# Attention and expert layer on one core: two buffers of turned x, batch 3 turned a slot sooner, x asked for ahead of row stores, batch 0's logits later, states @ w1 behind a slot's small pieces

## The chip, the cores and the metric

The kernel runs on one core of a Trainium2 chip. The metric is the device time of one execution in microseconds, from measurement outside the profile; the profile gives the span from the first to the last instruction of one profiled execution. The engines are TensorE (PE), VectorE (DVE), ScalarE (ACT), GpSimd (POOL) and SyncE (SP), which here issues nearly all the loads. Each engine works through its own queue in order and waits on semaphores for the others.

## The reference

```python
# x [8, 8, 512, 64], state [8, 8, 32, 64]   (batch, head, rows, D)
scores  = 0.125 * x @ state^T               # softmax over the 32 states
xread   = softmax(scores) @ state           # 512 rows per batch
scores2 = 0.125 * state @ x^T               # softmax over the 512 rows of x
sread   = softmax(scores2) @ x              # 32 rows per batch
tok = concat([xread, sread], axis=2).transpose(0, 2, 1, 3).reshape(8 * 544, 512)

logits = tok @ w_gate                       # 8 experts
e      = argmax(logits, axis=1)             # one expert per token
gate   = softmax(logits)[token, e]
out[token] = gate * (relu(tok @ w1[e]) @ w2[e])   # 512 -> 1024 -> 512
```

All of it is in float32. `w1` and `w2` are 2 MB for each expert.

## The kernel before

**What is computed.** The 512 x rows of a batch all go through one expert, the one that most of them choose, found at run time (`count`, `most`, `eb`, read by SP into a register with `expert_of`, and used as the address of the weight loads). The state rows are sorted by expert and go through their own rounds at the end; the token rows that did not choose their batch's expert are done in a branch behind all else. The x rows of the attention read are never formed: as `xread @ w1 = softmax @ (state @ w1)`, `states_w1` computes G = state @ w1 (PSUM tiles `pG`, 32 products for a batch, copied to `G` by ScalarE), and `up` multiplies the softmax weights, transposed (`aT`), by G (`ph`). `down` multiplies relu's output `hT` by w2 (`py`, 8 products of 128 x 512 for each of 4 chunks c); batches 2 to 7 use a seven-product scheme in `down_by_halves` and `up_by_halves`.

**The order of the work.** Everything is issued through one wrapper (line 48) that keeps each engine in program order, so every row of the profile shows L48 and has to be told apart by its tiles. The program's order is written by hand. `batch(b)` (line 1088) issues `down` of batch b and `up` of batch b+1; in between stand *slots* (`slots`, line 1129), into which the attention work of later batches is cut. One step of a slot issues one or two weight loads waiting in `lazy`, and one step of `attention()` (line 1063), which advances each running generator by one piece. In batch 0, `down` has slots 0 to 7: two for each chunk c, one behind the fourth `py` product of the chunk and one behind the chunk's store; `up(1)` has slots 8 to 11, `down(1)` slots 12 to 19. `between(c)` (line 1092) issues the `pG` of the next batch just ahead of a slot: with c = 2 in batch 0 ahead of slot 5, with c = 1 in batch 1 ahead of slot 15.

**The pieces.** `stages(b)` (line 335) is the attention of one batch, cut at each `yield`: turn x and the states (`turn_x`, `xt`; `turn_states`, `stT`, copied on by GpSimd); the gates of the states and first half of the scores (`states_gates`, `pg`; `scores`, `pc`); the second half, and the transposes and maxima on VectorE (`sx`, `mx`, `nm`); the exponentials (`a2`, `sx`); the transposed weights of the x read (`turn_read`, `aT`, which is also stored to `at_dram`); the transposed weights of the state read (`turn_write`, `pt`, `a2T`); the state rows and the logits of the x rows (`write_rows`, `pw`, `xs`; `logits_x`, `pl`, `lg`, and `route` on VectorE); the turned state rows (`turn_rows`, `pxs`); and the choice of the expert with the state rows' logits (`choose`, `count`, `pr`, `cnt`; `logits_s`, `pls`, `lgs`). From slot 0 on, a batch begins every third slot, batch 2 in slot 0. `begin()` (line 431) does batch 0's attention and batch 1's start, the latter in `beside()`, three steps taken between the `ph` of batch 0's last two chunks. `first()` (line 1034) is what is left of batches 0 and 1 and takes slots 0 to 6: `write_rows(0)`; `turn_write(1)`; `logits_x(1)`; `choose(1)` and the load of batch 1's w1; `write_rows(1)`; `turn_rows` of both; `logits_s` of both.

**Buffers.** Four PSUM banks (`bank`, tag p) are shared in turn by `py`, `ph`, `pG`, `pg`, `pt`, `pw`, `pl`, `pls`, `pxs` and `pr`; a new tile waits until the last reader of the bank it gets is done. The other four banks hold one `pc`. `xt` has one buffer for the whole of a batch, filled by two transposes; `x_nat` has three. `fetch_batch(b + 3)` at the end of `write_rows(b)` asks for x and the states three batches on, behind the four stores of the state rows to `srow`. SP waits, for each DMA it issues, for the one eight earlier.

Of the kernel before, what the change touches and what calls it, by code (L numbers as in the profile page):

```python
# [9 lines left out]
FP32 = mybir.dt.float32  # L10
# [10 lines left out]
def kernel(  # L21
# [34 lines left out]
    B, H, S, D = x.shape  # L56
# [142 lines left out]

    NB = 8  # L200

    def turn_x(b, xt, h):
        dve.transpose(xt[:, h].rearrange("p h c u t -> p (h c u t)"),
                      x_nat[b][:, h].rearrange("p h c d -> p (h c d)"))

    def turn_states(b, copy):

# [17 lines left out]
    def scores(b, xt, pc, g):  # L225

        for u in range(2):
            for q in range(4):
                for i in range(4):
                    pe.matmul(pc[ts(q, 32), i, ts(g, 128)], lhsT=stT[b][ts(i, 32), 2 * q + g, u ^ (i % 2), :],  # L230
                              rhs=xt[ts(i, 32), 2 * q + g, :, u, :],
                              start=(u == 0), stop=(u == 1), skip_group_check=True)

    def turn_scores(pc, sx, i):
# [37 lines left out]
    def new_pc():  # L272
        return ps_c.tile([128, 4, 512], FP32, tag="c", name="pc")

    def new_xt():
        return att.tile([128, H, NC, 2, 32], FP32, tag="xt", bufs=1, name="xt")

    def new_sx():
        return att.tile([128, 4, NB, NS], FP32, tag="sx", bufs=2, name="sx")
# [16 lines left out]
    def write_rows(b):  # L296

        _, _, s2, a2T = soft[b]
        pw = bank("pw")[:, 0:128].rearrange("p (g d) -> p g d", g=2)
        for g in range(2):  # L300
            for c in range(NC):
                for q in range(4):
                    pe.matmul(pw[ts(q, 32), g], lhsT=a2T[:, g, c, ts(q, 32)], rhs=x_nat[b][:, 2 * q + g, c, :],
                              start=(c == 0), stop=(c == NC - 1), skip_group_check=True)
        xs = rows_of[b] = att.tile([128, 2, D], FP32, tag="xs", bufs=2, name="xs")
        for g in range(2):
            act.activation(xs[:, g], pw[:, g], AF.Copy, scale=s2[:, g:g + 1])
        for q in range(4):
            sp.dma_start(out=srow[ts(b % 4, NS), b // 4, ts(q, 128)], in_=xs[ts(q, 32)].rearrange("p g d -> p (g d)"))
        fetch_batch(b + 3)  # L310

    def fetch_batch(b):
        if b < B:
            load_x(b, sp)
            load_states(b, sp, sp)

    def turn_read(b, i=ALL):
        if b not in aT:
            aT[b] = att.tile([128, 4, 2, 128], FP32, tag="aT", bufs=NE, name="aTe")[:]
        dve.transpose(aT[b][:, i].rearrange("p i g s -> p (i g s)"),  # L320
                      soft[b][0][:, i].rearrange("p i b n -> p (i b n)"))
        if i.stop == 4:
            sp.dma_start(out=at_dram[b], in_=aT[b].rearrange("p i g s -> p (i g s)"))

    def logits_x(b):
        pl = bank("pl")[:, 0:128]
# [7 lines left out]

    def stages(b):

        xt, sx = new_xt(), new_sx()
        turn_x(b, xt, slice(0, 4))
        turn_x(b, xt, slice(4, 8))
        turn_states(b, gp.tensor_copy)  # L340
        yield
        states_gates(b)
        pc = new_pc()
        scores(b, xt, pc, 0)
        yield
        scores(b, xt, pc, 1)
        for i in range(4):
            turn_scores(pc, sx, i)
        less_max(sx, ALL, gp)
        nm = write_max(pc)  # L350
        yield
        soft[b] = (sx,) + write_weights(pc, nm)
        exponential(sx, ALL)
        over_sum(sx, ALL, gp)
        yield
        turn_read(b)
        yield
        turn_write(b)
        yield
        write_rows(b)  # L360
        exps, gates = logits_x(b)
        yield
        exps()
        xsT = turn_rows(b)
        yield
        choose(b)
        logits_s(b, xsT)
        gates()

    def turn_rows(b):  # L370
# [4 lines left out]
        act.copy(xsT[:].rearrange("p q n -> p (q n)"), pt[:, 0:128])  # L375
        return xsT

    def logits_s(b, xsT):

        pl = bank("pls")[ts(b % 4, 32), 0:E]  # L380
        for q in range(4):
            pe.matmul(pl, lhsT=xsT[:, q, :], rhs=wg[:, q, :], start=(q == 0), stop=(q == 3), skip_group_check=True)
        dve.tensor_copy(out=lgs[ts(b % 4, 32), b // 4], in_=pl)
# [47 lines left out]
    def begin():  # L431
# [13 lines left out]
        most(0, pr)  # L445
        keep_warm(9)
        turn_states(0, act.copy)
        xt, sx = new_xt(), new_sx()
        turn_x(0, xt, slice(0, 4))
        e = expert_of(eb, 0)  # L450
        at_once(w1_parts(0, e, 2))
        load_x(1, sp)
# [1 line left out]
        sp.dma_start(out=wg[:], in_=moe_w_gate.rearrange("(c p) e -> p c e", p=128))  # L454
        at_once(w2_parts(0, e))
        fetch_batch(2)
        turn_x(0, xt, slice(4, 8))
        pc = new_pc()
        for g in range(2):
            scores(0, xt, pc, g)  # L460
# [27 lines left out]
        up(G, aT[0], hT, one, fs=far)  # L488
        up(G, aT[0], hT, two, fs=far)
        nm = write_max(pc)  # L490
        xt, sx = new_xt(), new_sx()
        turn_x(1, xt, slice(0, 4))
        turn_x(1, xt, slice(4, 8))
        turn_states(1, gp.tensor_copy)
        first_e = att.tile([1, 1], FP32, name="first_e")
        dve.tensor_copy(out=first_e[:], in_=eb[0:1, 0:1])
# [1 line left out]
        def beside():  # L498
            nonlocal nm, pc
            soft[0] += write_weights(pc, nm)  # L500
            states_gates(0)
            yield
            states_gates(1)
            pc = new_pc()
            scores(1, xt, pc, 0)
            yield

            pr = bank("pre")[:, 0:1]
            pe.matmul(pr, lhsT=ones_f[0:1].to_broadcast([1, 128]), rhs=first_e[:], start=True, stop=True)
            scores(1, xt, pc, 1)  # L510
            exps, gates = logits_x(0)
            dve.tensor_copy(out=eb[:, 0:1], in_=pr)
            for i in range(4):
                turn_scores(pc, sx, i)
            less_max(sx, ALL, dve)
            nm = write_max(pc)
            early.append(stages(2))
            next(early[0])
            yield
            exps()  # L520
            gates()
            count(0)
            turn_write(0)
            exponential(sx, ALL)
            soft[1] = (sx,) + write_weights(pc, nm)
            over_sum(sx, ALL, dve)
            turn_read(1)
            yield
# [505 lines left out]
    def first():  # L1034

        write_rows(0)
        yield
        turn_write(1)
        yield
        exps, gates = logits_x(1)  # L1040
        yield
        exps()
        choose(1)
        e1 = expert_of(eb, 1)
        at_once(w1_parts(1, e1))
        lazy.extend(w2_parts(1, e1))
        gates()
        yield
        write_rows(1)
        yield  # L1050
        xsT = [turn_rows(b) for b in range(2)]
        yield
        for b in range(2):
            logits_s(b, xsT[b])

    def advance(gens, which):
        for g in which:
# [5 lines left out]
    def attention():  # L1063

        gens, slot = [first()], 0
        while gens:
            b = 2 + slot // 3
            old, new = gens[:], slot % 3 == 0 and b < B
            begun = slot < 6
            if begun:  # L1070
                advance(gens, old[:1])
            if new:
                gens.append(early.pop() if early else stages(b))
                if b > 2:
                    next(gens[-1])
            advance(gens, old[1:] if begun else old)
            slot += 1
            yield
# [9 lines left out]
    def batch(b):  # L1088

        nonlocal G, hT  # L1090

        def between(c):
            nonlocal G
            if c == (1 if b else 2) and b + 1 < B:
                G = states_w1(new_G(), w1s[b + 1], stG[:, b + 1])
            yield
            if c == 1 and 0 < b < B - 2:
                lazy.extend(w1_parts(b + 2, expert_of(eb, b + 2)))
            yield

        def between_products(n):
            nonlocal G
            if n in (3, 4) and b + 1 < B:
                if n == 3:
                    G = new_G()
                states_w1(G, w1s[b + 1], stG[:, b + 1], (n - 3,),
                          lambda name: late["ps_t"].tile([128, 512], FP32, tag="t", bufs=2, name=name))
            yield
            if n == 4 and b + 2 < B:
                lazy.extend(w1_parts(b + 2, expert_of(eb, b + 2)))  # L1110
            if n == 5 and b + 1 < B:
                sums_of[b + 1] = up_sums(G, aT[b + 1])
            yield

        if b < NE:
            down(hT, w2s[b], store_batch(b), slots, between)
        else:
            down_by_halves(b, hT, w2s[b], slots, between_products)
        if 0 < b < B - 2:
            lazy.extend(w2_parts(b + 2, expert_of(eb, b + 2)))  # L1120
        if b + 1 in sums_of:
            hT = up_by_halves(G, aT[b + 1], sums_of[b + 1], new_hT(), slots)
        elif b + 1 < B:
            hT = up(G, aT[b + 1], new_hT(), insert=slots, at=(1, 3, 5, 7) if b + 1 < NE else (1, 3, 4, 5, 6, 7))
        if b == 0:
            e2 = expert_of(eb, 2)
            lazy.extend(w1_parts(2, e2) + w2_parts(2, e2))
# [127 lines left out]
```

## Time and profile before

| | us |
|---|---|
| median of 4 runs | 444.74 (444.41 to 445.6) |
| the profiled execution | 444.26 |
| its span | 440.0 |
| PE busy | 428.7 |
| DVE busy | 225.2 |
| POOL busy | 153.3 |
| ACT busy | 127.4 |

The profiled execution has 4.26 us around its span. The granted clock of TensorE has a mean of 0.997 of full speed. The DMA engines move 110 MB, 250 GB/s on the mean.

A row of the profile's timeline gives the start and the length in us, the engine, the line, the operation, and output tiles <- input tiles with their shapes; behind xN, N instructions are put together. Brackets hold the time that the engine had stood idle and what released it. In the list of waits, the columns are the total, the number of times and the longest. A busy share that is high over the whole span can hide where the idle time lies; the forty slices and the tables by stretch show that.

### The profile page before, as it was taken

To read this page: it belongs to the slowest core of one execution; us is meant where nothing else is said; L and a number is where in the kernel's file an instruction comes from. 1 tells how busy PE (TensorE), PEld (TensorE's weight loads), DVE (VectorE), ACT (ScalarE), POOL (GpSimd) and SP (SyncE) were. 2 spreads that over 40 slices of the span, in tenths; PEclk is the share of its full clock that TensorE was granted. 3 is DMA by queue.
4 is the path that set the end of the run, shared out by engine and by line. 5 is a ranking of instruction groups with operands and counts; after the bars stand their busy time and mean duration, and the time that the engine had idled before them with its cause. 6 is when DMAs were issued, how large, how long until landed. Compare 5 with 4: busy or idle time off the path is not lost.

```text
span 440.0 us, 10186 instructions
## 1 busy us (share of the span) xinstructions
PE 428.7 (97%) x3933; PEld 290.9 (66%) x3933; DVE 225.2 (51%) x482; ACT 127.4 (29%) x287; POOL 153.3 (35%) x143
## 2 busy tenths in 40 slices
PE   8899989999999999999999999999999999999995
PEld 7676544555555457786758677766867685768673
DVE  4667784787796657433505261523442370527151
ACT  1454233453343442212311241012340242025100
POOL 2010140412422431673327424534336253644231
PEclk9999999999999999999999999999999999999998
DMA  5990289565493454899999699779937998884211
GB/s 180 330 336 11 94 266 331 162 217 160 127 368 107 148 204 142 268 347 403 385 388 385 196 338 393 271 269 397 387 143 236 395 373 285 307 285 170 95 49 59
DMA packets 64514, 110.04 MB, mean 250 GB/s; under 512 B 12944, under 2 KB 22416, under 8 KB 64465
## 3 DMA queue, kind: packets, MB, share of 16 engines
q1 hardware_dynamic: 60240, 99.99, 65.9%
q0 software_dynamic: 2240, 7.08, 4.2%
q10 hardware_dynamic: 1984, 2.31, 1.5%
q8 instruction: 32, 0.52, 0.5%
q14 instruction: 18, 0.14, 0.1%
HBM read 94.15 MB, written 14.95 MB: 248 GB/s over the span
## 4 chain that ended last, share of the span: by engine, by line
PE 85%; DVE 9%; DMA 2%; SPq 1%; issue 1%; POOL 1%; ACT 1%; DVEq 0%; POOLq 0%
PE ph L48 22%; PE pD L48 10%; PE pX L48 10%; PE py L48 7%; PE pY L48 5%; PE pZ L48 5%; PE pgy L48 5%; PE pgh L48 5%; PE pW L48 5%; PE pG L48 3%; PE pc L48 3%; DVE sx L48 2%; DVE xt L48 2%; DMA st<-in_state_dram 2%; PE pt L48 1%; DVE sm L48 1%
## 5 line engine op out<-in xcount | busy, mean ns | idle before, releaser
L48 PE MATMUL py<-w2t,hT 128*128 128x512 f32 x128 | 59.0, 604 | 0.0
L48 DVE TENSOR_TENSOR hT<-ph,hT 128x512 f32<-128x512 f32 x50 | 34.6, 692 | 40.7 <-PE ph L48 40.7
L48 POOL TENSOR_TENSOR Ta<-w2t,Ta 128x1024 f32<-128x1024 f32 x12 | 30.6, 2546 | 46.6 <-PE pD L48 26.7
L48 PE MATMUL pX<-w2t,hT 128*128 128x256 f32 x192 | 43.7, 381 | 0.0
L48 PEld LDWEIGHTS pX<-w2t,hT 128*128 128x128 f32 x192 | 36.2, 190 | 6.4 <-issue 1.7
L48 PEld LDWEIGHTS py<-w2t,hT 128*128 128x128 f32 x128 | 23.0, 189 | 25.6 <-issue 24.9
L48 DVE SCALAR_TENSOR_TENSOR yh<-pY,gw,yh 128x256 f32<-128x256 f32 x24 | 10.0, 478 | 54.3 <-PE pY L48 47.8
L48 ACT ACTIVATE hT<-ph 128x512 f32<-128x512 f32 (+2 forms) x50 | 22.9, 462 | 41.0 <-PE ph L48 41.0
L48 PE MATMUL ph<-aTl,G 128*128 128x256 f32 (+1 forms) x112 | 33.8, 444 | 0.0
L48 PE MATMUL ph<-aTe,G 128*128 128x128 f32 (+2 forms) x128 | 30.4, 388 | 1.4 <-DVE aTe L48 1.2
L48 ACT ACTIVATE yh<-pX,gw 128x256 f32<-128x256 f32 x36 | 14.4, 473 | 53.8 <-PE pX L48 52.6
L48 POOL DMA_DIRECT2D out_dram<-yh x23 | 16.8, 731 | 33.5 <-DVE yh L48 16.9
L48 POOL TENSOR_TENSOR sx<-sx,mx 128x1024 f32<-128x1024 f32 x6 | 11.5, 1912 | 47.1 <-DVE mx L48 47.1
L48 ACT ACTIVATE hT<-hT 128x512 f32<-128x512 f32 x30 | 18.9, 630 | 30.7 <-DVE hT L48 30.7
L48 PEld LDWEIGHTS ph<-aTl,G 128*128 128x128 f32 x112 | 20.6, 190 | 9.6 <-issue 7.7
L48 PEld LDWEIGHTS ph<-aTe,G 128*128 128x128 f32 x128 | 18.8, 191 | 10.2 <-issue 6.7
L48 ACT COPY G<-pG 128x512 f32<-128x512 f32 x32 | 17.0, 591 | 23.9 <-PE pG L48 23.9
L48 PE MATMUL pY<-Ta,Sa 128*128 128x256 f32 x96 | 22.2, 384 | 0.0
L48 POOL COPY stT<-stT 64x512 f32<-64x512 f32 x7 | 4.2, 606 | 51.5 <-DVE first_e L48 20.7
L48 PE MATMUL pZ<-Tb,Sb 128*128 128x256 f32 x96 | 22.1, 383 | 0.0
L48 PEld LDWEIGHTS pY<-Ta,Sa 128*128 128x128 f32 x96 | 17.8, 190 | 6.4 <-issue 3.4
L48 POOL TENSOR_TENSOR Tb<-w2t 128x1024 f32<-128x1024 f32 x6 | 14.2, 2371 | 22.2 <-issue 22.2
(176 smaller groups left out, 745.3 us busy)
## 6 DMA issues: line engine op xcount, KB each, us to landing
s<-in_moe_w_dram SPq DMA_DIRECT2D x192, 256.0 KB, 6.0
w2t<-in_moe_w_dram SPq DMA_DIRECT2D x32, 512.0 KB, 7.0
w1t<-in_moe_w_dram SPq DMA_DIRECT2D x28, 512.0 KB, 6.2
x_nat<-in_x_dram SPq DMA_DIRECT2D x16, 512.0 KB, 6.5
out_dram<-yh POOLq DMA_DIRECT2D x23, 256.0 KB, 5.2
at_dram<-aTl SPq DMA_DIRECT2D x6, 512.0 KB
w1t<-in_moe_w_dram SPq DMA_DIRECT2D x2, 1024.0 KB
out_dram<-y ACTq DMA_DIRECT2D x8, 256.0 KB, 6.2
```

Source lines behind the costliest of these rows:

```text
L48: ins = getattr(self.engine, name)(*args, **kw)
```

## The change

The change moves work; the instructions are nearly the same.

1. `xt` is two half tiles instead of one whole, with one pair in the attention pool for even batches, and one for odd batches in tiles (`Sa`, `Sb`) that batches 2 and up use later. Turning a batch no longer has to wait for the scores of the batch before it.
2. Batch 3 is turned in slot 2 instead of slot 3, behind the transposed weights of batch 1 on VectorE's queue.
3. `write_rows` asks for x and the states three batches on ahead of the four row stores; the store of batch 1's `aT` moves from `turn_read(1)` to behind `write_rows(0)`.
4. In `beside()`, `logits_x(0)` moves one step later, ahead of `turn_write(0)`; `count(0)` moves to slot 0, behind `write_rows(0)`; batch 2 is turned after the exponentials.
5. The two `logits_s` of batches 0 and 1 write to one PSUM bank, in different partitions of it.
6. In `between(c)`, the `pG` products stand behind the slot's pieces instead of ahead of them (slot 5 for batch 1, slot 15 for batch 2).

```diff
-    def turn_x(b, xt, h):
-        dve.transpose(xt[:, h].rearrange("p h c u t -> p (h c u t)"),
-                      x_nat[b][:, h].rearrange("p h c d -> p (h c d)"))
+    def turn_x(b, xt, k):
+
+        dve.transpose(xt[k][:].rearrange("p h c u t -> p (h c u t)"),
+                      x_nat[b][:, ts(k, 4)].rearrange("p h c d -> p (h c d)"))
...
-    def new_xt():
-        return att.tile([128, H, NC, 2, 32], FP32, tag="xt", bufs=1, name="xt")
+    def new_xt(b):
+
+        return [(att, ffn)[b % 2].tile([128, 4, NC, 2, 32], FP32, tag=("xt0", "xt1", "Sa", "Sb")[2 * (b % 2) + k], name="xt")
+                for k in range(2)]
...
+        fetch_batch(b + 3)
         for q in range(4):
             sp.dma_start(out=srow[ts(b % 4, NS), b // 4, ts(q, 128)], in_=xs[ts(q, 32)].rearrange("p g d -> p (g d)"))
-        fetch_batch(b + 3)
...
-        if i.stop == 4:
-            sp.dma_start(out=at_dram[b], in_=aT[b].rearrange("p i g s -> p (i g s)"))
+        if i.stop == 4 and b != 1:
+            keep_read(b)
+
+    def keep_read(b):
+        sp.dma_start(out=at_dram[b], in_=aT[b].rearrange("p i g s -> p (i g s)"))
...
-    def logits_s(b, xsT):
-
-        pl = bank("pls")[ts(b % 4, 32), 0:E]
+    def logits_s(b, xsT, pl):
+
+        pl = pl[ts(b % 4, 32), 0:E]
...
             scores(1, xt, pc, 1)
-            exps, gates = logits_x(0)
             dve.tensor_copy(out=eb[:, 0:1], in_=pr)
             for i in range(4):
                 turn_scores(pc, sx, i)
             less_max(sx, ALL, dve)
             nm = write_max(pc)
-            early.append(stages(2))
-            next(early[0])
-            yield
-            exps()
-            gates()
-            count(0)
+            yield
+            exps, gates = logits_x(0)
             turn_write(0)
             exponential(sx, ALL)
             soft[1] = (sx,) + write_weights(pc, nm)
+            exps()
+            early.append(stages(2))
+            next(early[0])
+            gates()
             over_sum(sx, ALL, dve)
             turn_read(1)
...
         write_rows(0)
+        keep_read(1)
+        count(0)
         yield
...
+        pl = bank("pls")
         for b in range(2):
-            logits_s(b, xsT[b])
+            logits_s(b, xsT[b], pl)
...
+            if slot == 2:
+                early.append(stages(3))
+                next(early[0])
...
             if new:
-                gens.append(early.pop() if early else stages(b))
-                if b > 2:
-                    next(gens[-1])
+                if not early:
+                    early.append(stages(b))
+                    next(early[0])
+                gens.append(early.pop())
...
         def between(c):
             nonlocal G
+            yield
             if c == (1 if b else 2) and b + 1 < B:
                 G = states_w1(new_G(), w1s[b + 1], stG[:, b + 1])
-            yield
```

More of the change, by code (lines that the diff above doesn't have):

```diff
@@ L230, in scores @@
                     pe.matmul(pc[ts(q, 32), i, ts(g, 128)], lhsT=stT[b][ts(i, 32), 2 * q + g, u ^ (i % 2), :],
-                              rhs=xt[ts(i, 32), 2 * q + g, :, u, :],
+                              rhs=xt[q // 2][ts(i, 32), 2 * (q % 2) + g, :, u, :],
                               start=(u == 0), stop=(u == 1), skip_group_check=True)
@@ L335, in stages @@
     def stages(b):
-        xt, sx = new_xt(), new_sx()
-        turn_x(b, xt, slice(0, 4))
-        turn_x(b, xt, slice(4, 8))
+        xt, sx = new_xt(b), new_sx()
+        for k in range(2):
+            turn_x(b, xt, k)
         turn_states(b, gp.tensor_copy)
@@ L366, in stages @@
         choose(b)
-        logits_s(b, xsT)
+        logits_s(b, xsT, bank("pls"))
         gates()
@@ L447, in begin @@
         turn_states(0, act.copy)
-        xt, sx = new_xt(), new_sx()
-        turn_x(0, xt, slice(0, 4))
+        xt, sx = new_xt(0), new_sx()
+        turn_x(0, xt, 0)
         e = expert_of(eb, 0)
@@ L456, in begin @@
         fetch_batch(2)
-        turn_x(0, xt, slice(4, 8))
+        turn_x(0, xt, 1)
         pc = new_pc()
@@ L490, in begin @@
         nm = write_max(pc)
-        xt, sx = new_xt(), new_sx()
-        turn_x(1, xt, slice(0, 4))
-        turn_x(1, xt, slice(4, 8))
+        xt, sx = new_xt(1), new_sx()
+        for k in range(2):
+            turn_x(1, xt, k)
         turn_states(1, gp.tensor_copy)
```

## The prediction

> **What bounds the kernel now.** I read the page's busy table first, then its forty slices, then TensorE's list of waits.
>
> ```profile
> PE 428.7 (97%) x3933; PEld 290.9 (66%) x3933; DVE 225.2 (51%) x482; ACT 127.4 (29%) x287; POOL 153.3 (35%) x143
> ...
> PE   8899989999999999999999999999999999999995
> ```
>
> TensorE (PE) works for 428.7 of 440.0 us; no other engine passes 51%. So a microsecond comes off only where PE stands still, and one put in front of PE is paid in full. Busy time by stretch puts the idle time at the start (3.8 us in 0–30), the last 5 us, 1.5 in 60–65, 0.2 in 70–75 and 0.6 in 75–80; from 80 to 435 it is 0.1 in all. The list of PE's waits names the middle ones:
>
> ```profile
> PE pg L48 <- DVE stT L48: 1.0, 1, 1.0
> PE pg L48 <- POOL stT L48: 0.9, 2, 0.5
> PE pl L48 <- ACT xs L48: 0.6, 1, 0.6
> PE pt L48 <- ACT G L48: 0.2, 1, 0.2
> ```
>
> The timeline of PE shows where they lie; the brackets hold the idle time ahead of a row.
>
> ```profile
> 60.74 1.10 PE L48 MATMUL pw<-x_nat,a2T 128*32 128x64 f32 x64
> 62.86 0.20 PE L48 MATMUL pg<-wg,stT 64*32 64x8 f32 x2 [1.01 <-DVE stT L48]
> 63.53 0.27 PE L48 MATMUL pg<-wg,stT 64*32 64x8 f32 x14 [0.47 <-POOL stT L48]
> ...
> 71.72 1.15 PE L48 MATMUL pt<-ident,a 128*128 128x128 f32 x8 [0.16 <-ACT G L48]
> ...
> 79.56 0.65 PE L48 MATMUL pl<-aTl,gst 128*32 128x128 f32 x16 [0.64 <-ACT xs L48]
> ```
>
> The first is late because batch 3's x is fetched late. SyncE's waits from 30 to 60 us, and VectorE's timeline, say why:
>
> ```profile
> SPq L48 <- DVE s L48: 19.8, 1, 19.8
> ...
> 59.78 2.34 DVE L48 STREAM_TRANSPOSE xt<-x_nat 128x1024 f32<-128x1024 f32 x2
> 62.05 0.66 DVE L48 STREAM_TRANSPOSE stT<-st 64x512 f32<-64x512 f32 x1
> ```
>
> SP stood 19.8 us behind the store of batch 1's weights (released as `aTe` ends); the load of x(3), queued behind it and four row stores, was issued at 52.98 and landed at 58.1 and 60.1.
>
> **The basis.** The sum is made against the profiled execution: 444.26 us, 440.0 of span and 4.26 around it. It stands 0.48 below the median of 444.74; the sum is carried to the median at the end.
>
> **Two stalls that go.** (1) Slot 4. The store of batch 1 now stands behind the loads in `write_rows(0)`, and the loads ahead of the row stores, so x(3) is asked for when SP is free, at about 42.5, into DMA engines 0 to 15% busy from 40 to 50 us. Its own 5.1 and 6.5 us from issue to landing put it at 49 to 50. VectorE turns it right behind `aTe(1)` (48.68 + 1.25) and the two small `s`, and is through (2.34 + 0.66) at about 53, ten microseconds before `pg` needs it. The second half buffer of xt removes the wait on batch 2's scores. The step from 60.74 to the next py at 64.72 shrinks by the two idle times and the gap between: pw usually lasts 0.92 to the next row (110.90 to 111.82), pg 0.20 (83.87 to 84.07), pc 1.00 (84.07 to 85.07), so py could follow at 62.86. **−1.86.**
>
> (2) Slot 5. pG stood in front of the transposes and made them wait for ACT's four G copies; its own weights arrived late too (the second half's w1 piece landed at 68.98). From 68.36 to the py at 73.80 is 5.44; the pieces alone are pxs 0.40, pt 1.03, pc 1.00 and 32 pG 1.88 (127.31 to 129.19) = 4.31. With pG behind them, w1 has 2.4 us more to arrive, and G is only needed at the next `ph`. **−1.13.** The load of w1 is issued about 1 us later than now, landing near 70.0 against a need at about 70.8 less what (1) pulls forward; a lateness of up to 2 us would vanish in wait (4) below.
>
> **Three waits that come.** I compared, wait by wait, the order of the built programs; four PSUM banks go round for everything but the scores, so whoever is moved also moves the bank that the next tile gets.
>
> (3) Slot 1. `count(0)` now stands in slot 0, and its bank is held until VectorE's copy `cnt`, which is queued behind `aTe(1)`. So the second `pg` bank of batch 2 becomes the one that ScalarE's first a2T copy frees, where it was freed by y:
>
> ```profile
> 46.16 0.69 ACT L48 ACTIVATE y<-py,gw 128x512 f32<-128x512 f32 x1
> 46.88 0.38 ACTq L48 DMA_DIRECT2D out_dram<-y  x1
> 47.64 1.07 ACT L48 COPY a2T<-pt 128x512 f32<-128x512 f32 x2 [0.79 <-PE pg L48]
> ```
>
> y ends at 46.85, before PE comes to pg at 46.93; the first of the two copies ends at about 48.2. Then 15 small pg (0.25) and pc (1.08) remain, and py starts at 49.2 (if the copy starts as soon as the store is issued, 47.26) to 49.55, where it was 48.28. **+1.1** (0.95 to 1.27; 0 if another bank turns out free).
>
> (4) Slot 6. The two `logits_s` now share a bank, and the second's first product waits for VectorE's copy `lgs` of the first. That copy is queued behind the whole softmax head of batch 3 and the turning of batch 4:
>
> ```profile
> 73.91 1.44 DVE L48 STREAM_TRANSPOSE sx<-pc 128x256 f32<-128x256 f32 x4 [5.88 <-PE pc L48]
> 75.38 1.22 DVE L48 TENSOR_REDUCE mx<-sx 128x32 f32<-128x1024 f32 x1
> 76.52 1.22 DVE L48 TENSOR_REDUCE nm<-pc 128x2 f32<-128x1024 f32 x1
> 77.77 0.85 DVE L48 TENSOR_SCALAR nm<-nm 128x2 f32<-128x2 f32 x1
> 78.53 2.36 DVE L48 STREAM_TRANSPOSE xt<-x_nat 128x1024 f32<-128x1024 f32 x2
> 80.82 0.66 DVE L48 STREAM_TRANSPOSE stT<-st 64x512 f32<-64x512 f32 x1
> 81.41 0.30 DVE L48 COPY lgs<-pls 32x8 f32<-32x8 f32 x2
> ```
>
> Copy one ends 7.7 us after pc. PE gets to the second product after pG (1.9) and eight py (3.7), 5.7 after pc with pls's own start: it waits 2.0. The slot was 77.43 to 80.13 = 2.70, of which 0.81 was today's wait on the bank of `xs`, which goes; it becomes 1.89 + 2.0 + the 0.1 around a wait = 3.97. **+1.27.** If x(4) lands late (about 74 to 74.6, wanted at 74.8), all of this moves back by as much. A price of 0 for the shared bank would make the step −0.81.
>
> Against this step speaks the Trainium skill, "PSUM — Partial Sum Buffer", section "PSUM bank collisions raise a hardware error": engines may use one bank at once if in different 32-partition quadrants, and the two groups here are in different ones. By that rule no wait is needed and the step is the −0.81; the built order however has the wait, so I count it. No run here yet shows two groups in one bank.
>
> (5) Slot 15 (batch 2, c = 1): pG for batch 3 now stands behind pw and pl, so its fourth bank is pl's, which is freed by VectorE's transpose `lg`:
>
> ```profile
> 127.31 1.95 PE L48 MATMUL pG<-w1t,stG 64*32 64x512 f32 x32
> 129.19 1.10 PE L48 MATMUL pw<-x_nat,a2T 128*32 128x64 f32 x64
> 130.10 0.62 PE L48 MATMUL pl<-aTl,gst 128*32 128x128 f32 x16
> ...
> 131.29 0.26 DVE L48 STREAM_TRANSPOSE lg<-pl 128x128 f32<-128x128 f32 x1
> ```
>
> lg is queued behind xt and stT of batch 7 and ends at 131.55, whatever PE does. PE would reach the bank at 127.31 + 0.92 + 0.55 + 0.94 = 129.72, waits to 131.6, has 0.9 of pG left and starts py at 132.5 where it was 130.65. **+1.85** (1.6 to 2.0, by where the four products overlap; 0 if the bank is another's).
>
> **What costs nothing.** Batch 0's `pl` and `count` are as many products as before. Their VectorE route moves behind `nm` and joins a chain that keeps its length; `aTe(1)` ends no later, and its reader pl(1) comes at 52. Turning x in two calls was two calls already. Row stores now queue behind x loads; srow's reader, the sort of the state rows, comes in slots after 20. The exps of batch 7 (ScalarE 131–133) start up to 0.5 us earlier, ahead of the G copies, whose reader `ph` is over 6 us off. From 130 to 434 PE does not stop, so nothing there can give back or take what happened earlier.
>
> **Sum.** −1.86 − 1.13 + 1.1 + 1.27 + 1.85 = **+1.23**: 445.5 for an execution like the profiled one, **446.0** for the median. Its own range is +0.4 to +2.1 (446.85).
>
> **The rivals.**
> - *Other side, a new wait that does not bind.* One mechanism: VectorE's queue reaches the freeing instruction before PE. It needs `lgs` within 5.7 us after pc where the rows give 7.7, or `lg` by 129.7 where they give 131.55. For: VectorE is at 51% overall. Against: its rows from 73.9 to 82 follow without a gap. One of (4), (5) gone: 1.23 − 2.1 or − 1.85 = −0.9 or −0.6, 443.9 to 444.1. Faster than 0.2% (0.89 us, about what tells from no change here) from the point where the waits (3) to (5) together fall below 2.9 of their 5.0 (1.1 + 2.1 + 1.85), since 3.8 of stalls go against them.
> - *All three vanish:* only the old stalls go, −1.86 − 1.13 − 0.81 = −3.8: 440.9. For: every producer has idle time somewhere. Against: three queues would all have to be early.
> - *A late transfer:* w1 or x(4), asked for behind eight other DMAs while the DMA engines are full (65–75 us), lands 1 to 2 us later than its need beyond wait (4): +2.2 to +3.2, 447 to 448. For: a margin of under 1 us; against: wait (4) covers the first 2 us of w1.
> - *No change:* stall (1) stays, because x(3) lands after 55 despite the earlier issue: then also 446 to 448; SP's 19.8 us in one wait speak against it.
>
> **How the numbers follow.** Chances: my sum 0.62, one wait missing 0.17, all missing 0.06, late transfer 0.15. My sum spreads to both sides of +0.89: about 0.45 of it slower, 0.17 within. One wait missing gives half within, half faster. So faster 0.14, same 0.26, slower 0.60. The range leaves out the vanishing of all three and half of the late transfers: 443.9 to 447.3.
>
> **What will show it.** In the new trace: no idle ahead of pg near 62; pG behind pc in slot 5; a wait of pg on ACT's a2T near 47 (1.2 us); a wait of pls on DVE's lgs of about 2; a wait of pG on DVE's lg of about 1.9 near 130. The prediction is wrong if any of the last three is absent, or if a wait on a DMA stands beside them.

## The result, and the profile after

The changed kernel takes 445.86 us (median of 52 runs), the kernel before 444.42 (78 runs): a ratio of 1.0029, with a 95% interval of 1.0021 to 1.0038. That is +1.3 us (0.9 to 1.7), where +1.23 was forecast. Repeated later in the rounds of other kernels (run e12 below), it gave 1.0033 (1.0017 to 1.0049).

The profiled executions show this badly: 444.08 us after and 444.26 before, spans of 439.9 and 440.0. The profiled execution of the changed kernel is the shortest of its runs (spans of 439.9 to 443.4, median 441.8). So the two traces are compared by steps and not by their ends. First the page's busy and slice lines of the changed kernel, then TensorE's (PE's) list of waits:

```profile
PE 427.9 (97%) x3933; PEld 290.0 (66%) x3933; DVE 225.1 (51%) x482; ACT 127.8 (29%) x287; POOL 153.5 (35%) x143
...
PE   8899998999999999999999999999999999999995
```

```profile
PE pls L48 <- DVE lgs L48: 1.3, 1, 1.3
PE pG L48 <- DMA w1t<-in_moe_w_dram: 1.2, 1, 1.2
PE pG L48 <- DVE lg L48: 0.9, 1, 0.9
PE pg L48 <- ACT a2T L48: 0.9, 1, 0.9
PE pg L48 <- POOL stT L48: 0.4, 1, 0.4
```

The two waits of `pg` on batch 3's `stT`, that of `pl` on `xs` and that of `pt` on G are gone; three new waits stand in their place, on the three releasers that were named. Their idle times, 0.9, 1.3 and 0.9 us, are below the forecast 1.2, about 2 and about 1.9; the lengths of the slots, below, show the whole cost. The wait on w1t belongs to the opening, at 12 us, and comes and goes from execution to execution. The timeline of PE has the places:

```profile
45.56 0.23 PE L48 MATMUL pg<-wg,stT 64*32 64x8 f32 x2
46.67 0.27 PE L48 MATMUL pg<-wg,stT 64*32 64x8 f32 x14 [0.88 <-ACT a2T L48]
...
61.35 0.27 PE L48 MATMUL pg<-wg,stT 64*32 64x8 f32 x16
...
68.61 2.52 PE L48 MATMUL pG<-w1t,stG 64*32 64x512 f32 x32
71.07 3.70 PE L48 MATMUL py<-w2t,hT 128*128 128x512 f32 x8
...
76.39 0.32 PE L48 MATMUL pls<-wg,xsT 128*32 128x8 f32 x5 [1.28 <-DVE lgs L48]
...
126.74 1.90 PE L48 MATMUL pG<-w1t,stG 64*32 64x512 f32 x18
129.58 1.09 PE L48 MATMUL pG<-w1t,stG 64*32 64x512 f32 x14 [0.94 <-DVE lg L48]
130.59 3.70 PE L48 MATMUL py<-w2t,hT 128*128 128x512 f32 x8
```

In slots 1, 6 and 15 a group of products stands still in its middle; in slot 4, at 61.35, `pg` now runs through. In slot 15 the row ahead of the bracket belongs to the wait too: its 18 products take 1.90 us, where all 32 take 1.95 in the kernel before. SyncE's timeline shows why slot 4 runs through: x(3) is asked for at 41.09 instead of 52.98. And x(4) is asked for at 62.12, behind batch 1's w1 and the first piece of its w2, instead of at 66.26.

```profile
41.09 0.94 SPq L48 DMA_DIRECT2D x_nat<-in_x_dram  x2
...
59.45 1.97 SPq L48 DMA_DIRECT2D w1t<-in_moe_w_dram  x4
61.61 0.38 SPq L48 DMA_DIRECT2D w2t<-in_moe_w_dram  x1
62.12 0.98 SPq L48 DMA_DIRECT2D x_nat<-in_x_dram  x2
```

The slots in question each lie between two groups of eight `py`, so the differences between the starts of these groups give the slots' lengths. The starts that bound slots 1, 4, 5, 6 and 15, first in the kernel before:

```profile
42.42 3.70 PE L48 MATMUL py<-w2t,hT 128*128 128x512 f32 x8
...
48.28 3.70 PE L48 MATMUL py<-w2t,hT 128*128 128x512 f32 x8
...
57.13 3.68 PE L48 MATMUL py<-w2t,hT 128*128 128x512 f32 x8
...
64.72 3.70 PE L48 MATMUL py<-w2t,hT 128*128 128x512 f32 x8
...
73.80 3.70 PE L48 MATMUL py<-w2t,hT 128*128 128x512 f32 x8
...
80.13 3.70 PE L48 MATMUL py<-w2t,hT 128*128 128x512 f32 x8
...
123.68 3.70 PE L48 MATMUL py<-w2t,hT 128*128 128x512 f32 x8
...
130.65 3.70 PE L48 MATMUL py<-w2t,hT 128*128 128x512 f32 x8
```

and in the changed kernel, beside those at 71.07 and 130.59 above:

```profile
41.08 3.68 PE L48 MATMUL py<-w2t,hT 128*128 128x512 f32 x8
...
47.87 3.70 PE L48 MATMUL py<-w2t,hT 128*128 128x512 f32 x8
...
56.71 3.68 PE L48 MATMUL py<-w2t,hT 128*128 128x512 f32 x8
...
62.55 3.70 PE L48 MATMUL py<-w2t,hT 128*128 128x512 f32 x8
...
78.10 3.70 PE L48 MATMUL py<-w2t,hT 128*128 128x512 f32 x8
...
121.64 3.70 PE L48 MATMUL py<-w2t,hT 128*128 128x512 f32 x8
```

| step | before, us | after, us | difference | forecast |
|---|---|---|---|---|
| opening, to the first py (slot 0 follows it) | 37.86 | 36.40 | −1.46 | 0 |
| slot 0 | 4.56 | 4.68 | +0.12 | 0 |
| slot 1 | 5.86 | 6.79 | +0.93 | +1.1 |
| slots 2 and 3 | 8.85 | 8.84 | −0.01 | 0 |
| slot 4 | 7.59 | 5.84 | −1.75 | −1.86 |
| slot 5 | 9.08 | 8.52 | −0.56 | −1.13 |
| slot 6 | 6.33 | 7.03 | +0.70 | +1.27 |
| slots 7 to 14 | 43.55 | 43.54 | −0.01 | 0 |
| slot 15 | 6.97 | 8.95 | +1.98 | +1.85 |
| from there to PE's last product | 304.30 | 304.30 | 0.00 | 0 |

The slots add up to +1.40 us. The opening stands by itself: 1.15 us of its 1.46 lie ahead of the first `pg` (26.84 and 25.69), where both programs are the same on PE and executions differ by as much; the other 0.31 is a gain that the prediction did not have (see the last section).

Slots 5 and 6 depend on when batch 1's w1 lands in the execution that was profiled. In both of these it is late: TensorE's weight loads (PEld) for `pG` wait for it, in the kernel before

```profile
69.02 0.57 PEld L48 LDWEIGHTS pG<-w1t,stG 64*32 64x32 f32 x18 [0.50 <-DMA w1t<-in_moe_w_dram]
```

and in the changed kernel

```profile
69.23 0.57 PEld L48 LDWEIGHTS pG<-w1t,stG 64*32 64x32 f32 x18 [0.45 <-DMA w1t<-in_moe_w_dram]
```

The kernel of e7 below has the order of before in these slots, and w1 came in time there: slots 5 and 6 take 8.52 and 6.34 us, where they took 9.08 and 6.33. With the changed order and w1 in time (e1 and e3) they take 7.94 and 7.61. So with w1 in time in both, the difference is −0.58 and +1.27, +0.69 together; with w1 late in both it is the +0.14 of the table.

### The profile page after: what moved, and what is told of

It reads as the page before. It is cut to its first block, busy times and chain, and to the rows that moved or that the text cites. A ratio compares the mean times of both kernels' runs of the same rounds, so it can differ in the third digit from the quotient of the medians.

```text
span 439.9 us, 10188 instructions
## 1 busy us (share of the span) xinstructions
PE 427.9 (97%) x3933; PEld 290.0 (66%) x3933; DVE 225.1 (51%) x482; ACT 127.8 (29%) x287; POOL 153.5 (35%) x143
## 4 chain that ended last, share of the span: by engine, by line
PE 88%; DVE 8%; issue 1%; ACT 1%; POOL 1%; ACTq 0%; POOLq 0%; DVEq 0%
PE ph L48 22%; PE pD L48 10%; PE pX L48 10%; PE py L48 9%; PE pY L48 5%; PE pZ L48 5%; PE pgy L48 5%; PE pgh L48 5%; PE pW L48 5%; PE pc L48 3%; PE pG L48 3%; DVE xt L48 2%; PE pt L48 1%; DVE sx L48 1%; PE pw L48 1%; DVE nm L48 1%
## 5 line engine op out<-in xcount | busy, mean ns | idle before, releaser
L48 DVE TENSOR_TENSOR hT<-ph,hT 128x512 f32<-128x512 f32 x50 | 34.6, 692 | 40.7 <-PE ph L48 40.7
```

The source lines that it names most:

```text
L48: ins = getattr(self.engine, name)(*args, **kw)
```

## The experiments

All were timed in rounds against the kernel before on the same chip; a difference in us is the ratio's part of 444.4. "Time outside the span" is the device time less the span of the same execution. The theory: PE is the bound, and each new wait hangs on a PSUM bank whose reader stands late in another engine's queue. The rivals: the shared bank or the late place of `pG` costs by itself; the next bound (w1, stT) takes over.

**e1: batch 0's count copied by ScalarE.**

```diff
-    def count(b):
+    def count(b, copy=None):
...
-        dve.tensor_copy(out=cnt[:, b], in_=pr)
+        (copy or dve.tensor_copy)(out=cnt[:, b], in_=pr)
...
-        count(0)
+        count(0, lambda out, in_: act.copy(out, in_))
```

> The changed kernel, but ScalarE instead of VectorE copies batch 0's count out of its PSUM bank in slot 0, so the bank is free some 4 us earlier; same work otherwise. Theory (each new wait hangs on a bank whose reader is queued late): the 0.9 us wait of pg on ScalarE's a2T in slot 1 goes, nothing else changes, about 1.0 us off the changed kernel: +0.3 us against the kernel before (ratio 1.0007). Rival (the wait is only the first of two, and VectorE or the transfer of w1 sets the next one): the time stays at +1.3 us, and the 1 us shows up as a longer wait in slots 5 or 6.

Measured: 0.9995 (0.9972 to 1.0017), −0.2 us. The interval holds the forecast 1.0007 and leaves out the changed kernel's 1.0029. The trace says where: slot 1 lasts 5.75 us (6.79 in the changed kernel), the wait of `pg` on a2T is gone, and slots 5 and 6 together stay at 15.55 in both. Within slots 5 and 6 the wait of `pls` is longer (1.9 us for 1.3), but slot 5 is shorter by as much, since w1 came in time here; none of slot 1's gain moved on to a later wait. The bank's late reader was the whole cost of slot 1.

**e2: the two lgs copies ahead of batch 4's turning on VectorE.**

```diff
-            begun = slot < 6
+            begun = slot < 7
```

> The changed kernel, with the two state logits of slot 6 recorded ahead of the turning of batch 4, so that on VectorE's queue the two copies lgs stand ahead of xt and stT (3.0 us); TensorE's order and the shared bank stay as they are. Theory (VectorE's queue is the cost, not the shared bank): the wait of pls on lgs shrinks from 1.3 to 0.2 or 0.3 us (a hand-over from engine to engine), about 1.1 us off: +0.2 us against before (1.0005). Rival (the shared bank itself costs, whoever is early): the wait stays above 1 us and the time at +1.3 us.

Measured: 0.9977 (0.996 to 0.9993), −1.0 us against before, so some 2 us off the changed kernel, more than the 1.1 expected. The shared bank is still there, and the wait falls from 1.3 to 0.2 us: VectorE's order is the cost, and the bank's own price is the 0.2 of a hand-over. The profiles of e4, e10 and e11, which have the same order in these slots, put the gain at 1.6: slots 5 and 6 take 13.93 or 13.94 us there and 15.55 in the changed kernel. The 1.1 came from the changed kernel's first profile, where the wait on lgs was shorter because w1 was late. The execution of e2 that was profiled is no guide to its time: w1's last piece landed at 71.68 and slot 5 took 9.94 us, where seven of the ten other profiles with pG behind slot 5's pieces have 7.94.

**e3: lg ahead of batch 7's xt and stT in slot 15.**

```diff
+            if slot == 15:
+                advance(gens, old)
+                old = []
             if new:
```

> The changed kernel, with batch 7 turned behind batch 5's logits in slot 15, so that lg stands ahead of xt and stT (3.0 us) on VectorE; pG stays behind the slot's pieces. Theory: the wait of pG on lg in slot 15 (0.94 us shown, 2.0 us on the clock of TensorE's products) goes, no new wait of pg on stT in slot 16, 1.9 us off: -0.6 us against before (0.9987). Rival (the late place of pG is the cost by itself, or stT of batch 7 is late now): the time stays at +1.3 us or a wait of about 1 us on stT takes its place.

Measured: 0.9997 (0.9978 to 1.0016), −0.1 us, and this theory fell. The wait on lg is gone, but three others took its place, on ScalarE's G copies and then on stT; the timeline of PE in e3:

```profile
127.56 1.95 PE L48 MATMUL pG<-w1t,stG 64*32 64x512 f32 x32
130.79 3.70 PE L48 MATMUL py<-w2t,hT 128*128 128x512 f32 x8 [1.28 <-ACT G L48]
...
135.07 0.20 PE L48 MATMUL pg<-wg,stT 64*32 64x8 f32 x2 [0.47 <-DVE stT L48]
135.74 0.27 PE L48 MATMUL pg<-wg,stT 64*32 64x8 f32 x14 [0.47 <-POOL stT L48]
```

pG's banks are freed by the G copies, and these now stand behind the exponentials on ScalarE: `a` and `sx` from 127.87 to 130.26, the copies from 130.14. Slots 15 and 16 last 14.47 us together, 13.89 in the changed kernel and 11.91 before. The waits on stT, in slot 16, come from e3's own later turning; slot 15 by itself takes 8.32 us, for 8.95 in the changed kernel and 6.97 before. So as long as `pG` stands late, freeing its bank alone only shows the next wait; with `pG` back in its early place (e10) the slot takes 6.98. That the time still fell is not from the slots: the median span is 442.3 us, above before's 440.2, but the time outside the span is 1.8 instead of 4.1 us.

**e4: e1, e2 and e3 together.** The three edits above.

> The three edits of the runs before this one together: all that the change wins, without the three waits that it brought. Theory: the gains add up, 1.0 + 1.1 + 1.9 = 4.0 us off the changed kernel, -2.7 us against before (0.9939). Rival (a common next bound, such as w1 or x of batch 4 arriving late): less than half of the sum, -0.7 us or worse, with a wait on a transfer in slots 4 to 7.

Measured: 0.9923 (0.9897 to 0.995), −3.4 us. The size fits the expectation, for the wrong reason: slot 1 is 5.74 and slots 5 and 6 are 13.94 (15.41 before), but slots 15 and 16 cost 14.47 as in e3, and 2.3 us come from outside the span (1.8 against 4.1).

**e5: the early fetch and turning alone, on the kernel before.**

```diff
-        if i.stop == 4:
-            sp.dma_start(out=at_dram[b], in_=aT[b].rearrange("p i g s -> p (i g s)"))
+        if i.stop == 4 and b != 1:
+            keep_read(b)
...
+        fetch_batch(b + 3)
         for q in range(4):
             sp.dma_start(out=srow[ts(b % 4, NS), b // 4, ts(q, 128)], in_=xs[ts(q, 32)].rearrange("p g d -> p (g d)"))
-        fetch_batch(b + 3)
...
         write_rows(0)
+        keep_read(1)
...
+            if slot == 2:
+                early.append(stages(3))
+                next(early[0])
```

(with the two buffers of half tiles of xt, and with the generators started from `early`, as in the change.)

> The kernel before with only the early fetch and turning: half tiles of xt in two buffers, batch 3 turned in slot 2, x asked for ahead of the row stores and batch 1's aT stored behind write_rows(0). Theory: the stall of pg in slot 4 (1.5 us of idle time, 1.9 with the gap) goes and no wait comes: -1.8 us against before (0.996). Rival (the earlier loads only move the wait to w1 of batch 1, which queues behind them): -0.5 us or less, with a longer wait of pG on w1 in slot 5.

Measured: 1.0022 (1.0009 to 1.0035), +1.0 us: the theory fell, the rival holds. Slot 4 gains 1.75 us (7.59 to 5.84) and slot 5 gives back 2.19 (9.08 to 11.27), or 2.75 against the 8.52 of e7, where w1 came in time: a loss of 0.4 or 1.0 in the two slots, and the measured interval is 0.4 to 1.6. PE's timeline in e5:

```profile
61.75 0.27 PE L48 MATMUL pg<-wg,stT 64*32 64x8 f32 x16
...
66.58 1.06 PE L48 MATMUL pG<-w1t,stG 64*32 64x512 f32 x8
68.17 1.05 PE L48 MATMUL pG<-w1t,stG 64*32 64x512 f32 x4 [0.53 <-DMA w1t<-in_moe_w_dram]
69.44 1.91 PE L48 MATMUL pG<-w1t,stG 64*32 64x512 f32 x20 [0.23 <-DMA w1t<-in_moe_w_dram]
```

PE comes to pG 1.8 us earlier, and w1's last piece lands at 69.40, where it was 68.98. With pG at the head of slot 5, w1's landing sets the time, so whatever is saved ahead of it is lost there. The early x pays only together with the later pG.

**e6: only batch 1's pG behind the pieces of slot 5.**

```diff
-            if c == (1 if b else 2) and b + 1 < B:
+            if c == 1 and b:
                 G = states_w1(new_G(), w1s[b + 1], stG[:, b + 1])
             yield
+            if c == 2 and not b:
+                G = states_w1(new_G(), w1s[b + 1], stG[:, b + 1])
```

> The kernel before with only batch 1's pG put behind the pieces of slot 5. Theory: the waits around pG go, 1.1 us off: -1.1 us (0.9975); pl in slot 6 then waits for lgs about as long as it waited for xs. Rival (pl's new wait on lgs takes it all back): 0.0 us, with a wait of pl of 1.5 us or more in slot 6.

Measured: 0.9992 (0.9973 to 1.0011), −0.4 us with an interval that holds both ends of the expectation: the time does not decide. In the trace slot 5 falls to 7.94 and slot 6 rises from 6.33 to 6.48, 1.0 off; `pl` waits 0.79 on lgs where it waited 0.64 on xs. Part of the 1.0 is w1, late in the profile of before and in time here: against e7's 14.86 for the two slots their 14.42 are 0.4 less, as the time has it.

**e7: only batch 2's pG behind the pieces of slot 15.**

```diff
-            if c == (1 if b else 2) and b + 1 < B:
+            if c == 2 and not b:
                 G = states_w1(new_G(), w1s[b + 1], stG[:, b + 1])
             yield
+            if c == 1 and b:
+                G = states_w1(new_G(), w1s[b + 1], stG[:, b + 1])
```

> The kernel before with only batch 2's pG put behind the pieces of slot 15. Theory: the wait on lg comes alone and is paid in full, +1.9 us (1.0043). Rival (TensorE gives it back in the 300 us that follow, or pl's earlier place lets VectorE's route run earlier): within 0.5 us of before.

Measured: 1.0045 (1.0026 to 1.0063), +2.0 us: slot 15 goes from 6.97 to 8.95 and nothing later gives it back. Part six of the change is two moves with opposite signs.

**e8: a bank for each of the state logits.**

```diff
-        pl = bank("pls")
         for b in range(2):
-            logits_s(b, xsT[b], pl)
+            logits_s(b, xsT[b], bank("pls"))
```

> The changed kernel with a bank for each of the two state logits, as before; VectorE's queue stays. Theory: the second pls runs at once, but pl behind pw now needs the bank that the first lgs copy frees; TensorE has about 1.2 us more to do before it gets there, so the wait shrinks from 1.3 to about 0.3 us: 0.9 us off, +0.4 us against before (1.0009). Rival (the shared bank is the whole cost): the wait is gone altogether, 1.3 us off, 0.0 us.

Measured: 1.0002 (0.9986 to 1.0018), +0.1 us, between the two expectations. In its trace slots 5 and 6 take 14.43 us (15.55 with the shared bank) and no wait is left in slot 6, but slot 5 was 0.73 longer than its shortest (`pG`'s weight loads waited 0.6 for w1), which gave VectorE the time. It does not decide; e2 does.

**e9: one GpSimd instruction more.**

```diff
+    spare = const.tile([128, 1], FP32)
+    gp.memset(spare[:], 0.0)
+
     soft, rows_of = {}, {}
```

> The changed kernel with one more GpSimd instruction, a memset of one number per partition that nobody reads, in its opening. In the runs so far, the time outside the span was 1.8 us in the two kernels whose GpSimd program is one instruction longer (lg ahead of xt in slot 15) and 4.1 us in all the others, the changed kernel and the one before among them. Theory (the length of GpSimd's program sets it, not what the slots do): the span stays and the time outside it falls from 4.1 to 1.8 us, -2.3 us against the changed kernel, -1.0 us against before. Rival (it belongs to the order of slot 15): 4.1 us stay outside, +1.3 us against before.

Measured: 0.9978 (0.9963 to 0.9993), −1.0 us, and 2.5 below the changed kernel in the same rounds (443.07 and 445.57). The median span is 441.25 (441.3 without the memset); outside it are 1.74 to 1.92 us in all twelve runs, against 4.0 to 4.6. An instruction that nobody needs saves 2.3 us.

**e10: the change without its three waits.** e1 and e2, and in `between`, as in the change for batch 0 and as before for batch 1:

```diff
             nonlocal G
+            if c == 1 and b:
+                G = states_w1(new_G(), w1s[b + 1], stG[:, b + 1])
             yield
-            if c == (1 if b else 2) and b + 1 < B:
+            if c == 2 and not b:
                 G = states_w1(new_G(), w1s[b + 1], stG[:, b + 1])
```

> The changed kernel without its three new waits: ScalarE copies the count, the state logits are recorded ahead of batch 4's turning in slot 6, and batch 2's pG stands ahead of slot 15's pieces again, while batch 1's stays behind those of slot 5. From the steps between py groups in the profiles so far: slot 0 +0.1, slot 1 -0.1, slot 4 -1.8, slots 5 and 6 -1.5, slot 15 0.0, and 0.3 to 1.1 in the opening: -3.8 us against before (0.9915). Rival (w1 of batch 1, asked for together with x of batch 4, lands too late once nothing else hides it): slots 5 and 6 give back 1 to 2 us, -2 us.

Measured: 0.9912 (0.9895 to 0.9929), −3.9 us: 440.37. From 28 us on, all that is left in PE's list of waits is

```profile
PE pg L48 <- POOL stT L48: 0.4, 1, 0.4
PE pls L48 <- DVE lgs L48: 0.2, 1, 0.2
```

and slots 1, 4, 5, 6 and 15 last 5.74, 5.84, 7.94, 5.99 and 6.98 us. The rival did not come: pG takes its 1.95 in slot 5 without a wait on w1.

**e11: e10 with e9's memset.**

> The run before this one with the one GpSimd memset more. Theory: both gains add, the span as in the run before this one and 1.8 us outside it: -6.1 us against before (0.9863). Rival (no effect of the extra instruction): equal to the run before this one.

Measured: 0.9859 (0.984 to 0.9878), −6.3 us: 437.92, the fastest of all. The two gains add.

**e12: the changed kernel again**, unaltered, in the rounds of e9 to e11.

> The changed kernel unaltered, on the same chip and in the same rounds as the three runs above, so that they can be set against it: +1.3 us against before (1.0029), 4.1 us outside the span.

Measured: 1.0033 (1.0017 to 1.0049), +1.5 us, 4.16 outside the span. Slot 5 lasts 7.94 here (8.52 in the first profile), and the wait of `pls` is 1.9 (1.3): what w1 loses, the wait on lgs hides, as the prediction said. Slots 5 and 6 make 15.55 in the first profile and 15.97 here; the 0.42 more lie in `pl` at the end of slot 6 (1.06 us for 0.64), where the granted clock was 0.64 from 78 to 79 us and 0.50 in the next.

## Why the prediction was right

- *The bound.* PE sets the time, and what is put in front of it is paid in full: e7's slot is 1.98 longer and its time 2.0, and from slot 15 to PE's last product the two kernels need the same 304.30 us.
- *Stall 1, slot 4:* forecast −1.86, measured −1.75. The mechanism holds, but e5 adds what the step did not say: without the later pG the gain is worth nothing, since w1 becomes the end of the wait. The prediction saw the lateness of w1 and put it into slots 5 and 6.
- *Stall 2 and wait 4, slots 5 and 6:* −1.13 and +1.27 forecast; −0.56 and +0.70 in the first profile. The sum, +0.14, is as forecast, but that hangs on w1, which was late in that execution as it had been in the profile of before (0.45 and 0.50 us). With w1 in time in both kernels, the wait on lgs costs the forecast +1.27, and stall 2 is worth −0.58: the other half of its 1.13 was the late w1 of one execution, which the step counted as gained for good. It also expected w1 to be asked for about 1 us later than before; it was 0.4 earlier (59.45 and 59.88). The terms of wait 4 make 3.99, not 3.97, which changes nothing.
- *Wait 3, slot 1:* +1.1 forecast, +0.93 measured, the lower end of the bound (49.2 less 48.28). The a2T copy started as the store's issue ended (45.51 + 0.38, and 45.94). The step left out the four products of `count(0)`, 0.12 us, which are now in slot 0 and were in the opening.
- *Wait 5, slot 15:* +1.85 forecast, +1.98 measured; alone (e7) the same 1.98.
- *The rivals.* None took over. The one on the other side needed VectorE to be early; e2 makes `lgs` early by hand, and its −1.0 us is what that rival said for it (−0.9). The rule on quadrants of a PSUM bank could not be tested, since the program's order makes PE wait for the first copy in any case; with that copy early the wait costs 0.2 us (e2).
- *What was missing.* The opening. That batch 0's logits move later was costed at nothing, because the products stay the same; it takes 0.3 to 1.4 us out of the opening, a stall that the waits on semaphores do not list.
- *What stays open.* The slots' +1.40 less the mean of that gain over the four profiles that show it, 0.9, make +0.5; with w1 in time in both kernels the slots make +1.95, and the whole +1.0. The measured interval is +0.9 to +1.7. How often w1 is late is known of the profiled executions alone: one of the two that keep all of before's order there (before, e7), and four of the eleven with `pG` behind slot 5's pieces; the times of e5 and e6 fit w1 in time better. If it mostly is in time, the forecast's +1.23 was met in part by luck: the opening's gain of 0.9, which it did not have, was set off for the larger part by the 0.55 by which stall 2 was too large; if not, some 0.8 us stay without an explanation. The granted clock is a small part at most: its mean is 0.9964 in the changed kernel's 66 executions and 0.9974 in the 82 of before, and the mean spans differ by 1.5 us; among the executions with 0.998 or more they are 440.8 (26) and 439.7 (46), 1.1 apart.

## What to carry to other kernels

When PSUM banks go round in a fixed order, moving a tile moves the bank of every tile behind it: list, for each, which instruction frees its bank and how much stands ahead of that one in its queue. A shared or late bank costs nothing if its reader is early, and moving the reader (one line, e1 and e2) is cheaper than moving the products; but look one wait further, because the next bank may hang on another engine (e3). A stall that one profile shows may be that execution's: look into other profiles of the same order before pricing it (w1 in slot 5). Try the halves of a change by themselves: here two halves of one part had opposite signs (e6, e7), and a third (e5) was slower alone and needed for the gain of the whole.

## What the runs showed of the hardware

**PE stands at one and the same instruction in the opening.** In the three other profiled kernels that keep the order of before there (e5, e6 and e7), the 14th of the 16 recorded `pl` products of batch 0 starts at 34.66, 34.62 and 34.46, however early PE comes to it; in e6:

```profile
32.96 0.63 PE L48 MATMUL pl<-aTe,gst 128*32 128x128 f32 x13
34.62 0.41 PE L48 MATMUL pl<-aTe,gst 128*32 128x128 f32 x3 [1.02 <-issue]
```

"Issue" means that no semaphore is to blame. In the kernel before, it is only seen in the row `pl` of 0.97 us for the usual 0.65. That product's weight load is the 962nd of PE's recorded instructions, loads and products counted; e2 has such a stall (0.46 us, in slot 5) at the 1986th, 1024 further on. The instruction queue moved 0.52 MB in 32 packets, 16 KB each, in both kernels, and 4 of them by 36 us before and 3 after. In the packed traces the third packet ends at 33.25, 33.25, 33.17 and 33.01 us in before, e5, e6 and e7, and the 962nd instruction starts 1.41 to 1.45 us later in all four; in the ten other profiles it comes later than that, and PE does not stop there. In e2 the 1986th starts 1.27 us behind the end of the seventh packet, four packets further on, and no other profile has it so soon behind that packet. With longer products ahead of it, as in the changed kernel, PE comes to this place later than 34.6 and does not stop; its first py then follows the first `pg` by 10.7 us in all ten profiles with this order, where it was 11.02, 11.57, 12.12 and 11.84 in before, e5, e6 and e7. The Trainium skill, "Runtime: NRT & Kernel Launch", section "Instruction fetch mechanics", says that an engine's instructions are refilled in blocks of 16 KiB, or 256 instructions, and that crossing a boundary is mostly hidden. The packet size agrees, and so do the 1024 instructions and four packets between the two places; the crossing is not hidden at these places, where the stall is 0.5 to 1.0 us. That the fetch is the cause is argued from these numbers, closely, but no run changes the fetch alone.

**The time outside the span has two values.** It is 4.0 to 4.7 us in every run of the kernel before, the changed kernel, and e1, e2, e5 to e8 and e10; and 1.7 to 1.9 in every run of e3, e4, e9 and e11. The traces record 254 GpSimd instructions in these four, those of its sequencer counted, and 253 in the others. e9 against e12 and e11 against e10 show that one more instruction does it. Why is not known; the second instruction queue moved 19 packets in these four and 17 or 18 in the others.
